# Attention on one core: the value products of a unit in five visits instead of nine, and the work beside them placed anew

## The chip, the cores and the metric

The kernel runs on one core of a Trainium2 chip. A core has a matrix engine (TensorE, in the profile PE, with its weight loads PEld), VectorE (DVE), ScalarE (ACT), GpSimd (POOL) and SyncE (SP, which issues most of the transfers). The engines run beside each other, each through its own instructions in their written order, and wait for each other through semaphores. The metric is the device time of one launch in microseconds (us).

## The reference

Attention over 8 batches and 8 heads of 576 positions with 64 columns, in which each query keeps its 32 largest scores, and then a layer of 8 experts over the 4608 positions, of which each position takes the one with the largest logit:

```
scores = scale * q @ k.T                        # scale = 1/8
kth    = 32nd largest score of each row
scores = where(scores >= kth, scores, -1e9)
attn   = exp(scores - max); attn /= sum(attn) + 1e-9
x      = attn @ v                               # heads side by side: 4608 x 512
logits = normalized(x) @ normalized(emb).T / tau
e      = argmax(logits); gate = softmax(logits)[e]
out    = gate * (relu(x @ w1[e]) @ w2[e])       # w1 512 x 1024, w2 1024 x 512
```

## The kernel before, in words

**Units and tiles.** Two batches and one head make a unit; there are 32 units (`NU`), eight to a pair of batches. A unit's 2 x 576 queries are nine tiles of 128 (tile 0 takes the last 64 queries of both batches, tiles 1 to 4 the first batch's others, 5 to 8 the second's), so there are 288 tiles. The attention stage is one loop, unrolled in Python, with one iteration `i` for each tile (line 1054), in which many steps for different tiles are issued; the order is written out by hand (`manual_schedule`), and each engine works through its part of it in that order. `m9` is `i % 9`; an iteration's number in the text is its `m9`.

**What an iteration issues.** On TensorE, in this order: the scores of tile i+2 (`nat`, L189: four matmuls of 288 columns, eight for a tile 0); in some iterations the expert columns of a unit (`expert_part`, L648); one chunk of the unit that was finished nine iterations ago (`chunk`, L885: the scores once more, but turned, so that keys are on the partitions, with a term that lies below zero for all keys under the threshold; chunk 4 of a unit holds the last keys of both batches and is issued in iteration 4 with twice the matmuls, its bf16 ones ending with 64 columns of weights); the value products (`av`, L898); and a piece of an early expert block. On ScalarE: L826 (sign against a first bound, with a count), L849 (`r`, what lies under the threshold), L794 (`xs`, the scores out of PSUM), L886 (`w`, the exponential of the chunk), and two times a unit L916 (`ob`, the copy of the finished products out of PSUM). On VectorE: eight maxima of L801 and the steps of L813 to L820 on them for the bound, L840 and L841 for the threshold. On GpSimd: L832 (one for each tile), and the splitting of queries and keys in two parts (L677, L679).

**Value products.** `av(u, b, c)` multiplies the weights `w` of chunk c of batch b with the values: 18 matmul instructions of 64 columns of weights and 73 columns (64 values, a one for the sum, 8 expert columns), which add up in one PSUM tile `po`. What is issued in one iteration is called a visit. Ten products a unit stand in nine visits, by the table `AVS` (lines 1049 to 1051): one in each iteration, two in iteration 6. The sums of batch 0 end in iteration 5 and are copied by `norm` in iteration 6, those of batch 1 end in iteration 0 and are copied in iteration 1. `winp`, nine constants that L841 reads on VectorE, is cut out of the same tile `po` (line 616).

**Expert columns.** `expert_part(u)` multiplies a unit's values with the expert embeddings (ten matmuls of 16 columns); `VES` lists the iterations in which it is issued, `load_vt` loads its input five iterations earlier into one of two buffers (`vt`), and `keep_ve` copies the kept result (`ves`) into the unit's values.

**Early expert blocks.** Once the positions of a pair of batches have been sorted to experts, 128 of an expert's positions can be worked through beside the attention. There are eight such blocks (`EARLY`), four of the first pair and four of the second, each with 17 pieces: one to turn the gathered rows (L473), eight up (L485) and eight down (L494).

**The planner.** It adds up for each iteration what it holds TensorE, ScalarE and GpSimd to be used (`used`, in ns) and carries what exceeds `SLOT` = 2950 as `debt`. A piece is placed where `spare("pe", 860)` finds room: debt, used and 860 within 2950. A visit counts 790, iteration 4's chunk 690 more, expert columns 1000. So pieces stand in all iterations but 4, 6 and those with expert columns. After the last tile, what is left of a segment is issued in one go (line 1109).

**Transfers.** SyncE issues them in order: `load` brings a unit's queries and keys, `stack` copies their split parts (`hi`, `lo`) to where the matmuls read them, `query_rows` and `top_row` build the second operand of the chunk, `load_v` and `load_vt` bring the values, and one expert weight transfer is issued in an iteration while there are any.

Of the kernel before, what the change touches and what calls it, by code (L numbers as in the profile page):

```python
# [10 lines left out]
F32 = mybir.dt.float32  # L11
F32R = mybir.dt.float32r
# [8 lines left out]
B, H, S, D = 8, 8, 576, 64  # L21
N, DM, E, F = B * S, H * D, 8, 1024
P = 128
SH = S // 2
NBP = B // 2
NU = NBP * H
# [25 lines left out]
def attn_moe_kernel(ctx: ExitStack, tc: tile.TileContext, qk, vb, vt, emb, tau, w1, w2, out):  # L52
# [537 lines left out]
    with ExitStack() as sx:  # L590
# [36 lines left out]
                nc.vector.memset(v[HALF[b], 8 + b, D:D + 1], 1.0)  # L627
            vts.append(v)
        vtr, ves = {}, {}
        VES = [6 + (7 * u) // 2 for u in range(NU)]  # L630

        def load_v(u):
            v, src = vts[u % NV], vb[u].rearrange("p (c d) -> p c d", c=9)
# [8 lines left out]
        def expert_part(u):  # L642

            h, t = u % H, vtr.pop(u)
            ve = ps_t.tile([P, 2, 512], F32, name=f"ve{u}", tag="pt")[:, 0, 0:10 * E].rearrange(
                "p (b c e) -> p b c e", b=2, c=5)
            for c in range(5):
                nc.tensor.matmul(ve[:, :, c], t[:, c * P:(c + 1) * P],  # L648
                                 eB[:, h].rearrange("p (b e) -> p b e", b=2),
                                 start=True, stop=True)  # L650
            ves[u] = vp.tile([P, 2, 5, E], F32, name=f"ves{u}", tag="ves", bufs=20)
            nc.scalar.copy(ves[u], ve)

        def keep_ve(u):
# [9 lines left out]
        QH = QW // 2  # L664

        def load(u, h):

            lo = sp.tile([P, QH], F32R, name=f"lo{u}_{h}", tag="lo", bufs=3)
            hi = sp.tile([P, QH], F32R, name=f"hi{u}_{h}", tag="hi", bufs=3)
            nc.sync.dma_start(lo.bitcast(F32), qk[u][:, QH * h:QH * h + QH])  # L670
            stage[u, h] = (hi, lo)

# [172 lines left out]

        def shut(i):
            r = rt[i] = wk.tile([P, S], BF16, name=f"r{i}", tag="rt" if i % 9 == 0 else "r",
                                bufs=2 if i % 9 == 0 else 10)
            nc.scalar.activation(r, xss.pop(i), AF.Relu, bias=tall[:, i:i + 1], scale=-1.0)  # L849

        ws = {}
# [1 line left out]
        def chunk(u, b, c):  # L853

            qs, kh, kl = stacks[u]
            w = ws[u, b, c] = wk.tile([P, S], F32, name=f"w{u}_{b}_{c}", tag="w", bufs=3)
            ps = ps_t.tile([P, 1024], F32, name=f"pt{u}_{b}_{c}", tag="pt")
            cut = (256, 320)[b]
            ps = ps[:, 512 - cut:512 - cut + S]
            part = [(0, cut), (cut, S)]  # L860
            for bb in ([b] if c < 4 else (1, 0)):
                first, offs = [], []
                k0, kn = (c * P, P) if c < 4 else ((512, 64), (448, P))[bb]
                rows = slice(0, kn)
                tiles = [(rt[u * 9 + 1 + 4 * bb + t], negi, P) for t in range(4)]
                tail = (rt[u * 9], negt[:, 64 * bb:64 * bb + 64], 64)
                tiles = tiles + [tail] if bb == 0 else [tail] + tiles
                q0 = 0 if bb == 0 else 640
                for kk, qq, n in ((kh, qs[:, q0:q0 + S], P), (kl, qts[u, bb], 65)):
                    for h0, h1 in part:  # L870
                        first.append((ps[rows, h0:h1], kk[0:n, bb * S + k0:bb * S + k0 + kn],
                                      qq[0:n, h0:h1], kk is kh, False))
                off = ([], [])
                o = 0
                for r, ni, n in tiles:
                    for hf, (h0, h1) in enumerate(part):
                        lo, hi = max(o, h0), min(o + n, h1)
                        if lo < hi:
                            off[hf].append((ps[rows, lo:hi], r[:, k0:k0 + kn],
                                            ni[:, lo - o:hi - o]))  # L880
                    o += n
                for hf in range(2):
                    offs += [(*x, False, n == len(off[hf]) - 1) for n, x in enumerate(off[hf])]
                for o_, l_, r_, start, stop in first + offs:
                    nc.tensor.matmul(o_, l_, r_, start=start, stop=stop)  # L885
            nc.scalar.activation(w, ps, AF.Exp, scale=0.125)  # L886
# [143 lines left out]
        debt = {"pe": 0, "act": 0, "pool": 0}  # L1030
        used = {}

        ROOM = {"pe": 0, "act": 1500, "pool": 1000}

        def spare(k, n, more=0):
            if i >= ntile or debt[k] + used[k] + n <= SLOT + ROOM[k] + more:
# [8 lines left out]
        for s in sorted(k for k in plan if k < 0):  # L1045
            for f in plan.pop(s):
                f()
        ok = lambda j: 0 <= j < ntile
        AVS = {1: [(0, 0, 1, 0)], 2: [(0, 1, 0, 0)], 3: [(0, 2, 0, 0)], 4: [(0, 3, 0, 0)],
               5: [(0, 4, 0, 1)], 6: [(1, 0, 1, 0), (1, 4, 0, 0)], 7: [(1, 1, 0, 0)],  # L1050
               8: [(1, 2, 0, 0)], 0: [(1, 3, 0, 1)]}
        i = -1
        while i < ntile + 12 or sideq or later or bankq or early or squares or wq or mo["seg"] \
                or mo["epi"]:
# [5 lines left out]
                used["pe"] += 712 + 690 * (m9 == 4)  # L1060
                used["act"] += 531
            avs = []
            for b, c, st_, sp_ in AVS[m9]:
                uu = w_ - (m9 == 0)
                if 0 <= uu < NU:
                    used["pe"] += 790
                    avs.append((uu, b, c, bool(st_), bool(sp_)))
            norms = [(w_ - (m9 == 1), (m9 == 1) * 1)] if m9 in (1, 6) else []
            norms = [x for x in norms if 0 <= x[0] < NU]
# [36 lines left out]
            if mo["seg"] is not None and not ntile <= i < ntile + 10 and spare("pe", 860):  # L1106
                todo, epi, after = mo["seg"]
                keep = KEEP if mo["of"] == 8 and i < ntile + 15 else 0
                for _ in range(max(len(todo) - keep, 0) if i >= ntile + 9 else 1):
                    lastpe.append(todo.pop(0))  # L1110
                if not todo:
                    mo["seg"], mo["epi"] = None, (epi, after)
# [619 lines left out]
```

## Time and profile before

| | |
|---|---|
| median of three runs | 1338.67 us (1338.01 to 1341.87) |
| profiled execution | 1340.78 us, its span 1339.0 us |
| TensorE busy over the span | 1281.6 us (96%), mean granted clock 0.974 |
| VectorE, ScalarE, GpSimd busy | 967.0 us (72%), 964.1 us (72%), 846.1 us (63%) |
| moved by DMA | 196.65 MB, mean 147 GB/s |

The page's busy tenths, in 40 slices of 33.5 us, show the stages: VectorE and ScalarE fall off where the attention ends.

```profile
PE   7999999999989999999999999999998999999997
DVE  7999999798878887888988888798834234443240
ACT  5899999898878898988889988898424234443231
POOL 5788888798877777888877887876522212122111
PEclk6899999899889999999999999999999999999999
```

A digit is the busy share of a slice in tenths, and of PEclk the granted clock of TensorE in tenths of full speed. Until 43.5 us the clock was mostly at half. The attention stage lasts to about 950 us, and the experts' stage follows. A busy share is an average over work with different limits, and the ends of matmuls are modelled, so that the time from the start of one group to the start of the next is what a group takes of TensorE.

### The profile page before, as it was taken

The page shows a single profiled execution, that of the slowest core. Times are in us where ns is not written, and L with a number is a line of the kernel's source. Part 1 is how long each engine was busy: PE and PEld are TensorE (multiplying, and loading weights), DVE is VectorE, ACT ScalarE, POOL GpSimd, SP SyncE. Part 2 cuts the span into 40 slices and gives each one's busy share as a digit, 9 for nine tenths or more (in the row PEclk, how much of TensorE's full clock was granted, in tenths as well). Part 3 has the DMA queues.
Part 4 walks back from the last instruction along what each step waited for, and adds up shares of the span by engine and source line. Part 5 has one row for each costly group of instructions (what it writes and reads, how often), then busy time and mean ns, then how long its engine had stood idle before and what let it go on. Part 6 is the DMA issues. An engine that isn't in the chain of part 4 may idle for free. (4 is left out here: it accounts for less than half of the span.)

```text
span 1339.0 us, 40065 instructions
## 1 busy us (share of the span) xinstructions
PE 1281.6 (96%) x13111; PEld 1126.4 (84%) x13111; DVE 967.0 (72%) x5961; ACT 964.1 (72%) x1890; POOL 846.1 (63%) x1413
## 2 busy tenths in 40 slices
PE   7999999999989999999999999999998999999997
PEld 5899999888878888888888988788797888888886
DVE  7999999798878887888988888798834234443240
ACT  5899999898878898988889988898424234443231
POOL 5788888798877777888877887876522212122111
PEclk6899999899889999999999999999999999999999
DMA  6477556644444667455666756550563325553201
GB/s 180 127 201 221 134 129 166 176 132 118 108 102 116 201 184 235 121 156 134 182 176 188 219 146 159 135 163 23 168 210 123 124 88 180 182 181 132 88 29 37
DMA packets 141174, 196.65 MB, mean 147 GB/s; under 512 B 66791, under 2 KB 67079, under 8 KB 140818
## 3 DMA queue, kind: packets, MB, share of 16 engines
q1 hardware_dynamic: 132626, 170.62, 45.8%
q0 software_dynamic: 8192, 22.07, 4.9%
q8 instruction: 127, 2.08, 0.7%
q14 instruction: 229, 1.88, 0.5%
HBM read 116.34 MB, written 20.87 MB: 102 GB/s over the span
## 5 line engine op out<-in xcount | busy, mean ns | idle before, releaser
L801 DVE MAX8 ca<-xs 128x8 f32<-128x72 f32 x2304 | 498.8, 221 | 2.3 <-ACT xs L794 1.6
L832 POOL TENSOR_TENSOR y<-xs,s 128x576 f32<-128x576 f32 x288 | 370.0, 1285 | 102.7 <-ACT s L826 45.3
L898 PE MATMUL po<-v,w 128*64 128x73 f32 x5760 | 270.2, 234 | 14.8 <-ACT ob L916 7.5
L189 PE MATMUL sc<-st 128*128 128x288 f32 (+1 forms) x1280 | 271.5, 341 | 7.5 <-DVE st L753 3.8
L898 PEld LDWEIGHTS po<-v,w 128*64 128x64 f32 x5760 | 227.2, 138 | 39.8 <-ACT s L826 7.2
L826 ACT ACTIVATE s<-xs,ball 128x576 bf16<-128x576 f32 x288 | 223.5, 776 | 21.4 <-DVE ball L820 11.5
L849 ACT ACTIVATE r<-xs,tall 128x576 bf16<-128x576 f32 x288 | 223.6, 777 | 14.4 <-DVE jk L841 11.2
L189 PEld LDWEIGHTS sc<-st 128*128 128x128 f32 (+1 forms) x1280 | 193.7, 198 | 48.0 <-issue 27.9
L840 DVE MAX8 z<-y 128x8 f32<-128x576 f32 x288 | 214.3, 744 | 20.6 <-POOL y L832 20.5
L886 ACT ACTIVATE w<-pt 128x576 f32<-128x576 f32 x288 | 187.9, 653 | 37.2 <-PE pt L885 31.5
L794 ACT ACTIVATE xs<-sc 128x576 f32<-128x576 f32 x288 | 185.8, 645 | 20.1 <-PE sc L189 19.0
L885 PE MATMUL pt<-st 128*128 128x256 f32 (+3 forms) x640 | 144.9, 308 | 0.3 <-ACT xs L794 0.3
L885 PE MATMUL pt<-qt,st 65*128 65x256 f32 (+3 forms) x640 | 139.1, 299 | 0.0
L841 DVE SCALAR_TENSOR_TENSOR jk<-po,c,z 128x9 f32<-128x9 f32 x288 | 65.7, 228 | 86.8 <-PE po L898 55.4
L885 PE MATMUL pt<-negi,r 128*128 128x128 bf16 (+2 forms) x1312 | 128.1, 222 | 0.0
L414 POOL DMA_INDIRECT out_dram<-ys_w,wi x20 | 24.8, 1240 | 159.6 <-ACT ys_w L1298 57.2
L679 POOL TENSOR_TENSOR lo<-lo,hi 128x202 fp32r<-128x202 f32 x186 | 115.7, 622 | 15.5
L885 PEld LDWEIGHTS <-r 128*128 128x128 bf16 (+1 forms) x1632 | 88.8, 101 | 28.2 <-issue 6.8
L885 PEld LDWEIGHTS pt<-qt,st 65*128 65x128 f32 (+1 forms) x640 | 104.2, 188 | 0.3
L885 PEld LDWEIGHTS pt<-st 128*128 128x128 f32 (+1 forms) x640 | 100.9, 189 | 1.9 <-ACT xs L794 0.6
L1279 PE MATMUL ph_w<-xTh,w 128*128 128x448 f32 (+3 forms) x384 | 96.5, 332 | 5.8 <-ACT w L546 3.4
L1294 PE MATMUL py_w<-w,hh 128*128 128x512 f32 x320 | 100.0, 393 | 0.8 <-ACT ys L1298 0.8
(288 smaller groups left out, 2360.2 us busy)
## 6 DMA issues: line engine op xcount, KB each, us to landing
r<-in_w SPq DMA_DIRECT2D x128, 256.0 KB
fr<-in_w SPq DMA_DIRECT2D x28, 1024.0 KB
lo<-in_qk SPq DMA_DIRECT2D x62, 304.0 KB
st<-hi SPq DMA_DIRECT2D x124, 152.0 KB
st<-lo SPq DMA_DIRECT2D x93, 152.0 KB
vt<-in_vt SPq DMA_DIRECT2D x32, 320.0 KB
qt<-st SPq DMA_DIRECT2D x64, 144.0 KB
st<-hi SPq DMA_DIRECT2D x62, 136.0 KB
```

What stands on the lines that cost most here:

```text
L189: nc.tensor.matmul(sc[:, hf, :SH], qs[0:r, cols(b)], kk[0:r, b * S + hf * SH:b * S + (hf + 1) * SH], start=(n == 0), stop=(n == len(terms) ...
L679: nc.gpsimd.tensor_tensor(lo[:, c], lo[:, c].bitcast(F32), hi[:, c].bitcast(F32), ALU.subtract)
L794: nc.scalar.mul(xs.rearrange("p (a b) -> p a b", a=2), scs.pop(i)[:, :, :SH], BIG)
L801: return [lambda gi=gi: nc.vector.max(out=ca[:, 8 * gi:8 * gi + 8], in_=xs[:, gi * GW:(gi + 1) * GW]) for gi in range(G)]
L826: nc.scalar.activation(s1, xss[i], AF.Sign, bias=ball[:, i:i + 1], scale=-DOWN, accum_out=c1)
L832: nc.gpsimd.tensor_tensor(y2, xss[i], s1s.pop(i), ALU.mult)
L840: lambda: nc.vector.max(out=z[:, 16:24], in_=y2),
L849: nc.scalar.activation(r, xss.pop(i), AF.Relu, bias=tall[:, i:i + 1], scale=-1.0)
L885: nc.tensor.matmul(o_, l_, r_, start=start, stop=stop)
L886: nc.scalar.activation(w, ps, AF.Exp, scale=0.125)
L898: nc.tensor.matmul(o, w[:, q:q + 64], vc, start=start and n < 2, stop=stop and n in (8, 7 - b))
L1294: nc.tensor.matmul(py, hi[:, f, col:col + P], wi[:, f, :], start=(n == 0), stop=(n == 3 * (F // P) - 1))
```

## The change

The ten products of a unit stand in five visits: two in iteration 2, one in 3, two in 5, two in 7 and three in 0 (of the next nine iterations). The sums end in iterations 5 and 0 as before. The planner counts a visit's first product at 900 and each further one at 570, and TensorE may run 500 over its slot. In iterations 1, 6 and 8, two pieces of a segment are issued where both find room. The expert columns go into iterations 1, 6 and 8 as well, three in nine iterations until 17 units' results are kept ahead, then one in nine. Four buffer counts differ: `ves` 19 instead of 20, `hi` 2 instead of 3, `r` 9 instead of 10, `w` 4 instead of 3.

```diff
@@ -627,7 +627,12 @@
                 nc.vector.memset(v[HALF[b], 8 + b, D:D + 1], 1.0)
             vts.append(v)
         vtr, ves = {}, {}
-        VES = [6 + (7 * u) // 2 for u in range(NU)]
+        VES = []
+        while len(VES) < NU:
+            n = VES[-1] + 1 if VES else 6
+            while n % 9 not in (1, 6, 8) or len(VES) - max(0, (n + 2) // 9) >= 17:
+                n += 1
+            VES.append(n)
 
         def load_v(u):
             v, src = vts[u % NV], vb[u].rearrange("p (c d) -> p c d", c=9)
@@ -648,7 +653,7 @@
                 nc.tensor.matmul(ve[:, :, c], t[:, c * P:(c + 1) * P],
                                  eB[:, h].rearrange("p (b e) -> p b e", b=2),
                                  start=True, stop=True)
-            ves[u] = vp.tile([P, 2, 5, E], F32, name=f"ves{u}", tag="ves", bufs=20)
+            ves[u] = vp.tile([P, 2, 5, E], F32, name=f"ves{u}", tag="ves", bufs=19)
             nc.scalar.copy(ves[u], ve)
 
         def keep_ve(u):
@@ -666,7 +671,7 @@
         def load(u, h):
 
             lo = sp.tile([P, QH], F32R, name=f"lo{u}_{h}", tag="lo", bufs=3)
-            hi = sp.tile([P, QH], F32R, name=f"hi{u}_{h}", tag="hi", bufs=3)
+            hi = sp.tile([P, QH], F32R, name=f"hi{u}_{h}", tag="hi", bufs=2)
             nc.sync.dma_start(lo.bitcast(F32), qk[u][:, QH * h:QH * h + QH])
             stage[u, h] = (hi, lo)
 
@@ -845,7 +850,7 @@
 
         def shut(i):
             r = rt[i] = wk.tile([P, S], BF16, name=f"r{i}", tag="rt" if i % 9 == 0 else "r",
-                                bufs=2 if i % 9 == 0 else 10)
+                                bufs=2 if i % 9 == 0 else 9)
             nc.scalar.activation(r, xss.pop(i), AF.Relu, bias=tall[:, i:i + 1], scale=-1.0)
 
         ws = {}
@@ -853,7 +858,7 @@
         def chunk(u, b, c):
 
             qs, kh, kl = stacks[u]
-            w = ws[u, b, c] = wk.tile([P, S], F32, name=f"w{u}_{b}_{c}", tag="w", bufs=3)
+            w = ws[u, b, c] = wk.tile([P, S], F32, name=f"w{u}_{b}_{c}", tag="w", bufs=4)
             ps = ps_t.tile([P, 1024], F32, name=f"pt{u}_{b}_{c}", tag="pt")
             cut = (256, 320)[b]
             ps = ps[:, 512 - cut:512 - cut + S]
@@ -1030,7 +1035,7 @@
         debt = {"pe": 0, "act": 0, "pool": 0}
         used = {}
 
-        ROOM = {"pe": 0, "act": 1500, "pool": 1000}
+        ROOM = {"pe": 500, "act": 1500, "pool": 1000}
 
         def spare(k, n, more=0):
             if i >= ntile or debt[k] + used[k] + n <= SLOT + ROOM[k] + more:
@@ -1046,9 +1051,8 @@
             for f in plan.pop(s):
                 f()
         ok = lambda j: 0 <= j < ntile
-        AVS = {1: [(0, 0, 1, 0)], 2: [(0, 1, 0, 0)], 3: [(0, 2, 0, 0)], 4: [(0, 3, 0, 0)],
-               5: [(0, 4, 0, 1)], 6: [(1, 0, 1, 0), (1, 4, 0, 0)], 7: [(1, 1, 0, 0)],
-               8: [(1, 2, 0, 0)], 0: [(1, 3, 0, 1)]}
+        AVS = {2: [(0, 0, 1, 0), (0, 1, 0, 0)], 3: [(0, 2, 0, 0)], 5: [(0, 3, 0, 0), (0, 4, 0, 1)],
+               7: [(1, 0, 1, 0), (1, 4, 0, 0)], 0: [(1, 1, 0, 0), (1, 2, 0, 0), (1, 3, 0, 1)]}
         i = -1
         while i < ntile + 12 or sideq or later or bankq or early or squares or wq or mo["seg"] \
                 or mo["epi"]:
@@ -1060,10 +1064,10 @@
                 used["pe"] += 712 + 690 * (m9 == 4)
                 used["act"] += 531
             avs = []
-            for b, c, st_, sp_ in AVS[m9]:
+            for b, c, st_, sp_ in AVS.get(m9, []):
                 uu = w_ - (m9 == 0)
                 if 0 <= uu < NU:
-                    used["pe"] += 790
+                    used["pe"] += 570 + 330 * (not avs)
                     avs.append((uu, b, c, bool(st_), bool(sp_)))
             norms = [(w_ - (m9 == 1), (m9 == 1) * 1)] if m9 in (1, 6) else []
             norms = [x for x in norms if 0 <= x[0] < NU]
@@ -1106,7 +1110,8 @@
             if mo["seg"] is not None and not ntile <= i < ntile + 10 and spare("pe", 860):
                 todo, epi, after = mo["seg"]
                 keep = KEEP if mo["of"] == 8 and i < ntile + 15 else 0
-                for _ in range(max(len(todo) - keep, 0) if i >= ntile + 9 else 1):
+                two = m9 in (1, 6, 8) and len(todo) > 1 and spare("pe", 860)
+                for _ in range(max(len(todo) - keep, 0) if i >= ntile + 9 else 1 + two):
                     lastpe.append(todo.pop(0))
                 if not todo:
                     mo["seg"], mo["epi"] = None, (epi, after)
```

## Rows read from the trace of the kernel before

**Rows 1.** Busy time by stretch: from:to, length, PE PEld DVE ACT POOL (instructions), PEclk, DMA.

```profile
43.50:225.00 181.50, 181.30 (x2366) 164.82 (x2367) 172.64 (x1222) 169.96 (x348) 146.64 (x249) 1.00 0.61 163
225.00:376.00 151.00, 143.99 (x1786) 130.18 (x1786) 131.84 (x928) 134.49 (x282) 130.00 (x234) 0.93 0.54 137
376.00:918.00 542.00, 528.36 (x6370) 458.13 (x6366) 454.81 (x3201) 473.99 (x934) 437.44 (x759) 0.99 0.59 160
```

**Rows 2.** Busy time by stretch, of line L832 alone, one instruction a tile.

```profile
43.50:225.00 181.50, 80.94 (x63) 1.00 0.61 163
225.00:376.00 151.00, 60.37 (x47) 0.93 0.54 137
376.00:918.00 542.00, 211.98 (x165) 0.99 0.59 160
```

**Rows 3.** TensorE in order: start us, us, operation; a plain iteration, 45.7 to 48.0 us.

```profile
45.72 0.81 PE L189 MATMUL sc<-st 128*128 128x288 f32 x4
46.36 0.43 PE L885 MATMUL pt<-st 128*128 128x256 f32 x2
...
47.14 0.19 PE L885 MATMUL pt<-negt,r 128*128 128x64 bf16 x1
47.26 0.85 PE L898 MATMUL po<-v,w 128*64 128x73 f32 x18
48.04 0.80 PE L189 MATMUL sc<-st 128*128 128x288 f32 x4
```

**Rows 4.** TensorE in order: iteration 6, a tile 0's scores, expert columns.

```profile
56.16 1.49 PE L898 MATMUL po<-v,w 128*64 128x73 f32 x36
57.58 1.34 PE L189 MATMUL sc<-st 128*128 128x288 f32 x8
58.76 1.19 PE L648 MATMUL ve<-eB,vt 128*128 128x16 f32 x10
59.80 0.39 PE L885 MATMUL pt<-st 128*128 128x320 f32 x1
```

**Rows 5.** TensorE in order: chunk and visit of an iteration 4.

```profile
50.38 0.39 PE L885 MATMUL pt<-negi,r 128*128 128x128 bf16 x5
50.57 0.45 PE L885 MATMUL pt<-st 128*64 128x256 f32 x2
...
51.22 0.41 PE L885 MATMUL pt<-negi,r 128*64 128x128 bf16 x4
51.42 0.28 PE L898 MATMUL po<-v,w 128*64 128x73 f32 x1
```

**Rows 6.** TensorE in order: an up piece, its scores up to the chunk.

```profile
420.96 1.16 PE L485 MATMUL bu4e<-bxe,r 128*128 128x128 f32 x8
...
422.50 0.42 PE L885 MATMUL pt<-st 128*128 128x320 f32 x2
```

**Rows 7.** Waits over the span: who waited for whom, us, times, longest us.

```profile
DVE jk L841 <- PE po L898: 55.4, 85, 5.8
...
PE po L898 <- ACT ob L916: 7.5, 8, 2.3
...
PE po L898 <- DVE ca L801: 6.5, 9, 1.6
...
PE bte L473 <- DMA xge<-xd,tgl: 4.8, 1, 4.8
```

**Rows 8.** Busy time by stretch, where the clock fell and where it didn't.

```profile
251.70:262.00 10.30, 10.30 (x75) 9.28 (x75) 6.52 (x48) 8.91 (x21) 6.96 (x13) 0.50 0.69 176
330.00:337.00 7.00, 4.71 (x65) 4.21 (x64) 4.51 (x35) 4.78 (x9) 5.48 (x8) 1.00 0.12 26
337.00:347.30 10.30, 10.10 (x73) 9.18 (x72) 6.66 (x42) 6.69 (x14) 9.54 (x15) 0.50 0.57 140
500.00:900.00 400.00, 391.27 (x4708) 337.06 (x4709) 338.19 (x2380) 351.88 (x697) 332.96 (x578) 1.00 0.63 170
```

**Rows 9.** TensorE in order: the pieces after the last visit.

```profile
943.86 6.28 PE L494 MATMUL bde<-r,bhe 128*128 128x512 f32 x14
```

## The prediction

> **What bounds the kernel now.** The page's slices show VectorE near full to about 900 of 1339 us, the attention stage, and that is where the change lies. There I read first the busy time by stretch, then TensorE's own order of instructions, then the waits. In the three stretches of the attention stage [rows 1] TensorE is busy 181.3 of 181.5 us, 144.0 of 151.0 and 528.4 of 542.0; the count of L832, one for each tile, says how many iterations each holds [rows 2]: 63, 47 and 165. An iteration so takes 2.88, 3.21 and 3.28 us. Per iteration VectorE is busy for 2.74, 2.81 and 2.76 us and ScalarE for 2.70, 2.86 and 2.87. TensorE is the limit in the first and the third stretch, by only 0.14 us in the first. In the second its clock stood at half for two spells of 10.3 us [rows 8], one of them right after a stretch in which it was idle for 2.3 of 7 us; there ScalarE's 2.86 is what would be left.
>
> VectorE's longest wait inside the stage (jk L841 for po L898, 55.4 us in 85 times [rows 7]) is no cause: `winp`, which L841 reads, is cut from the tile that the visits write, so L841 of an iteration waits for that iteration's visits, and the next visit waits for L841. It shows who is late, TensorE.
>
> **The price of a visit.** A plain iteration runs from one scores group to the next in 2.32 us [rows 3]: scores 0.64, chunk 0.90, visit 0.78. In iteration 6 two visits stand back to back and take 1.42 [rows 4], so a second one adds 0.64. What an iteration without a visit takes the trace doesn't show; I put it together. The eight scores matmuls of a tile 0 take 1.18 [rows 4], 0.54 more than four: after a visit four take 0.64, so 0.10 of it is the visit's. The chunk's last matmul (64 columns) starts 0.78 after its first and the visit only 0.12 after that [rows 3]; without a visit I let the scores follow after 0.03, since inside the chunk of iteration 4 an fp32r matmul follows the bf16 ones with no gap (five of them from 50.38, the next at 50.57 [rows 5]). That gives 0.81 + 0.54 = 1.35, so a visit costs 0.97, and one that is merged into another saves 0.97 - 0.64 = 0.33. From below the saving is 0 (the scores could pay the same after a chunk), from above 0.33; I take 0.33, as every part of it is a row.
>
> Four visits a unit are merged: those of iterations 1, 4, 6 and 8 go into 2, 5, 7 and 0 (that of 6 was double already and stays double). For iteration 4 I count nothing: its chunk ends in matmuls with 64 columns of weights, and there the visit starts beside them (51.42, the last bf16 ones being issued from 51.22 [rows 5]), so it pays no way in, and the way out to the scores is still to be paid without it. So 3 x 0.33 = 1.0 us a unit.
>
> [...]
>
> **First stretch, 43.5 to 225 us.** Seven units at 25.93 us. Minus 1.0; plus the expert columns, one of which takes 1.04 (58.76 to 59.80 [rows 4]): three in nine iterations instead of two in seven, 0.43 more a unit, 0.45 us. 25.38 a unit is 2.82 an iteration, 0.08 above VectorE: 3.9 us saved, of which I take 3, two engines at nearly the same load never running quite at the larger one's. Ends: -3.2 (no saving, the columns paid) and +8.9 (VectorE's own 172.6).
>
> **Second stretch, 225 to 376.** The old list puts 12 expert parts here (76 to 114), the new one 6 (78, 80, 89, 98, 107, 116). TensorE loses 6 x 1.04 and 5.2 x 1.0 of its 144.0, some 132.6 us, and ScalarE's 134.5 is the floor. The copy of `po` (L916) and the first visit of the next half stood in the same iteration (1 and 6), and TensorE waited for it 7.5 us in 8 times, up to 2.3 [rows 7]; now an iteration lies between (copy 1, visit 2; copy 6, visit 7). One such wait came right ahead of the fall of the clock at 337 us [rows 8]. A fall costs half of 10.3, 5.15 us. But iterations without a visit or a piece also leave TensorE idle, by up to 2.9 - 1.35 = 1.5 us at once, so I let one of two falls stay: 134.5 + 5.1 + 3.8 for waits between ScalarE and the others = 143.4, 7.6 saved. Ends: 16.5 (the floor) and -5.2 (one fall more).
>
> **Third stretch, 376 to 918.** The merged visits give 18.3 x 1.0 = 18.3. Against that stand the pieces. By the planner's budgets the old kernel places one in seven iterations of nine (none in 4 and 6); the new one two in 1, 6 and 8 where a segment has two left, one in 3 and 4, none in 0, 2, 5 and 7. Worked through with its debts that is about 7.5 a unit, and all 136 end near iteration 285, so the seven down pieces that ran after the last visit [rows 9] and one more come in here: 8 x 0.87 = 7.0. An up piece with its scores takes 1.54 [rows 6], 0.90 over a plain iteration's scores, and a down piece much the same (fourteen of its matmuls, seven pieces, last 6.3 us, their end modelled: 0.87 to 0.90 each [rows 9]); standing without a visit, the 0.10 by which the scores start late is the piece's own. That is 0.10 for about 55 iterations (in 4 the chunk's end pays it, in 3 the visit): 5.5. Its way in from a bf16 chunk isn't shown: between 0 (fp32r after bf16 [rows 5]) and 0.19 (the 0.09 by which a visit starts late in rows 3, and 0.10 for a slow first matmul); I take 0.05, near the row without a change of weight columns: 2.7. The second of a pair costs what a piece cost. Two expert parts (125, 134) are new here: 2.1. So TensorE's work falls by 18.3 - 7.0 - 5.5 - 2.7 - 2.1 = 1.0 only. It also waited 13.6 us; the 4.8 for the first gathered block [rows 7] stay, and of the other 8.8, which are mostly visits that wait for the copy or for L841, I let 4 go. 5 saved. Ends: -16 (merging saves half, the way in 0.19, no wait gone) and +12 (no way in, all 8.8 gone).
>
> **The rest.** After the last visit TensorE did the seven down pieces (6.3 us [rows 9]) beside the last gate's chain on ScalarE, GpSimd and VectorE; taking them away shortens nothing, and it leaves TensorE idle there. 1.0 for the last unit's visits against a slower restart: 0. At the start, with the clock at half until 43.5 us, a third expert part falls into iteration 10: -1. The expert stage is not touched.
>
> At nothing I cost the buffers. `r` with nine: tile 6 of a unit takes the place of tile 5 of the unit before, read last two iterations earlier. `w` with four: in program order each is read ahead of the chunk that takes its place. `hi` with two: six iterations (17 us) lie between the copies out of it and its next writing on GpSimd; if they were late, GpSimd's products (L832) would queue behind. `vt` keeps two buffers while each third load is now issued an iteration before the matmuls that free its place, so SyncE waits there with the top rows behind it; these are due three iterations on. Without that cover it would be up to an iteration's 2.8 us, nine times.
>
> The three visits of iteration 0 last 0.78 + 2 x 0.64 = 2.06 us, and L841 of that iteration waits for them: they fit into VectorE's 2.74 if they start in its first 0.7. Where TensorE is the limit this costs nothing.
>
> **Sum.** 3 + 7.6 + 5 + 0 - 1 = 14.6 us. The profiled execution took 1340.78 (span 1339.0 and 1.8 around it); it is 2.1 over the median of the three runs, to which I apply the sum: 1338.67 - 14.6 = 1324.
>
> **The rivals.**
> The pieces eat it. The way in is 0.19 (7.7 more in 55 iterations), no wait goes (4) and VectorE and TensorE get into each other's way in the first stretch (3): 1324 + 14.7 = 1339, no change. For: the new price of a piece is the one thing no row shows. Against: bf16 to fp32r is free.
>
> All of it. VectorE's floor in the first stretch (5.9 more), ScalarE's in the second (8.9), no way in and no waits in the third (7.5): 1302. For: both large stops ahead of the falls hang on the copy that gets an iteration's distance. Against: 0.08 us between two engines.
>
> The clock. TensorE is busy almost throughout now [rows 1]; with the visits gone from four iterations of nine it stands idle where no piece is to be had, in the second stretch and in the 6 us after the last visit. Each fall takes 5.15 us; 2.8 more than I count eat the gain, 3.6 make it 0.3% slower; four give 1345. For: a stop of 2.3 us was enough ahead of 337. Against: from 500 to 900 us, with waits of up to 1.6 us [rows 7], it stayed whole [rows 8]. [...]
>
> Merging saves nothing. A visit by itself would cost no more than its 0.64 and the rest be the scores' and the chunk's own; then the first stretch pays 3.2 instead of gaining 3 and the third loses its 18.3: 1324 + 24.5 = 1348. Against: 1.42 is well under two times 0.78 plus two late starts [rows 3, 4]. [...]
>
> **Chances.** Forecast 0.48 (1316 to 1332), pieces 0.18, all of it 0.16, clock 0.13, no saving 0.05. A change under 0.3% (4 us) can't be told from none. Faster: 0.48 + 0.16 + 0.03 of the pieces = 0.67; same 0.15; slower 0.18. The range reaches from the second rival to just above the first: 1302 to 1341.
>
> **What would show it.** L898 still with 5760 matmuls, in five groups a unit; a double visit of 1.42 and a triple one near 2.06; scores of 0.54 right after a chunk. Iterations of about 2.82 in the first 63. No wait of `po` for `ob` over 1 us. Down pieces over before the last visit. One or no spell at half clock between 225 and 376 us. Wrong if scores or pieces after a chunk start 0.1 or more late, if L841's wait grows beyond its 55 us in the first stretch, or if the clock's mean falls below the 0.974 of now.

## The result, and the profile after

The changed kernel takes 1350.49 us (median of 6 runs, 1346.02 to 1352.41), the kernel before beside it 1340.27 (6 runs, 1337.86 to 1342.65): a ratio of 1.0075, 95% interval [1.0054, 1.0096]. It is 10 us slower where 14.6 faster was forecast, and lies above the range of 1302 to 1341. The profiled execution took 1352.41.

Busy time by stretch in the changed kernel, cut where the same tiles' products (L832, now L837) begin; columns as in [rows 1]:

```profile
44.44:224.58 180.14, 180.12 (x2399) 166.38 (x2399) 170.98 (x1215) 169.22 (x351) 145.93 (x249) 0.99 0.62 170
224.58:371.71 147.13, 132.46 (x1724) 118.18 (x1722) 131.64 (x927) 133.05 (x275) 130.20 (x237) 0.97 0.50 129
371.71:926.32 554.61, 530.78 (x6391) 463.80 (x6392) 454.52 (x3201) 473.66 (x938) 435.94 (x757) 0.98 0.58 158
```

The third of these stretches in the last kernel of the table below (a_nob_pad, an experiment):

```profile
374.91:911.01 536.10, 526.69 (x6392) 460.11 (x6392) 454.59 (x3202) 473.31 (x938) 436.46 (x756) 0.99 0.60 163
```

The same tiles give, for three kernels (the last is a_nob_pad), in us:

| | start | first | second | third | from there to the end |
|---|---|---|---|---|---|
| before | 43.48 | 181.64 | 151.56 | 541.73 | 420.57 |
| forecast change | +1 | -3 | -7.6 | -5 | 0 |
| after | 44.44 | 180.14 | 147.13 | 554.61 | 424.37 |
| after, both causes taken away | 44.78 | 182.48 | 147.65 | 536.10 | 416.39 |

Each measured row is one execution. The times of one kernel spread by 5 to 13 us; a_nob_pad's profiled execution was 3.9 us under the median of its kernel and that of the changed kernel 1.9 over.

The first two stretches gained, 5.9 us of the 10.6 forecast. The third lost 12.9, and TensorE's work in it hardly grew (530.8 against 528.4 [rows 1]): it stands still for 23.8 us instead of 13.6, and without the two causes for 9.4. What follows lost 3.8. The waits of the changed kernel (who, for whom, us, times, longest), in which the wait of `po` for `ob` [rows 7] is no longer found:

```profile
DVE jk L846 <- PE po L903: 69.8, 63, 6.5
...
PE pt L890 <- ACT xs L799: 20.6, 18, 3.3
...
PE pr L369 <- DVE ohba L233: 6.1, 1, 6.1
...
POOL hi L682 <- DMA qt<-tr: 5.8, 1, 5.8
...
POOL hi L682 <- DMA lo<-in_qk: 5.2, 5, 3.9
...
PE sc L189 <- DMA st<-lo: 4.1, 2, 3.8
```

The waits of TensorE and GpSimd for `st`, `lo` and `qt` took 7.9 us in the kernel before; here they take 20. One costly place, first in SyncE's queue of transfers (start, us until the last is issued, line, how many), then on TensorE, on GpSimd, and by stretch:

```profile
728.38 4.83 SPq L967 DMA_DIRECT2D r<-in_w  x7
733.32 1.78 SPq L705 DMA_DIRECT2D st<-hi  x3
735.20 1.35 SPq L705 DMA_DIRECT2D st<-lo  x2
```

```profile
738.80 2.00 PE L485 MATMUL bu0e<-bxe,r 128*128 128x128 f32 x16
744.58 1.31 PE L189 MATMUL sc<-st 128*128 128x288 f32 x8 [3.77 <-DMA st<-lo]
```

```profile
745.49 0.37 POOL L682 TENSOR_SCALAR hi<-lo 128x202 fp32r<-128x202 f32 x1 [3.88 <-DMA lo<-in_qk]
...
746.53 1.27 POOL L837 TENSOR_TENSOR y<-xs,s 128x576 f32<-128x576 f32 x1
```

```profile
724.00:740.00 16.00, 16.00 (x205) 14.79 (x204) 15.28 (x112) 15.73 (x35) 12.33 (x24) 1.00 0.77 204
740.00:746.10 6.10, 2.33 (x19) 2.17 (x18) 3.23 (x21) 3.13 (x8) 1.96 (x6) 1.00 1.05 315
746.10:749.50 3.40, 3.40 (x44) 3.02 (x42) 0.00 (x0) 1.94 (x4) 3.15 (x5) 0.50 1.01 367
```

Seven transfers of an expert's down weights, 256 KB each, go out in one go just ahead of the next unit's stack. They are issued from 728.38 us on, the stack's five from 733.32, and the DMA engines' share is 1.05 from 740.0 to 746.1; the scores of the unit's tile 0 wait 3.77 us for `st`, GpSimd stands 3.88 at a copy into `hi` with the products (L837) behind it, and the granted clock is 0.50 for the 3.4 us from 746.1. In the program such a burst comes from `weights`: the first up piece of a block issues whatever of its expert's weights still waits in `wq`, the down weights too, which nothing needs before the eight up pieces are done. The kernel before has bursts as well; the new places of the pieces move them to other iterations of the unit.

The largest of TensorE's waits listed above is not for `st` but for `xs`; 8.9 us of it are four waits in the third stretch. One of these comes after the burst at 592 us (seven transfers as well). GpSimd stands for 4.95 us at the copy of the kept expert columns into `v`, which the profile puts down to one of GpSimd's own transfers; its products follow late, and ScalarE and TensorE wait in their turn:

```profile
601.48 0.19 POOL L665 COPY v<-ves 64x8 f32<-64x8 f32 x1 [4.95 <-DMA lst<-enta,slotia]
604.11 0.78 ACT L831 ACTIVATE s<-xs,ball 128x576 bf16<-128x576 f32 x1 [4.81 <-POOL y L837]
607.00 0.53 PE L890 MATMUL pt<-st 128*128 128x256 f32 x2 [2.48 <-ACT xs L799]
```

In the third stretch GpSimd waits at this copy for some 20 us, against 4.3 in the kernel before.

The second place is in the expert stage, where no line was changed: TensorE's idle time ahead of an up matmul, and the branch of the first `Switch` (count, ns least/median/most, start), in the changed kernel, then the branch in the one before:

```profile
999.49 0.55 PE L1266 MATMUL ph<-xTh,w 128*128 128x256 f32 x1 [4.07 <-issue]
```

```profile
L1733 PEldq COMPARE_BRANCH  x1: 5267/5267/5267, 993.9 to 993.9; - x1
```

```profile
L1728 PEldq COMPARE_BRANCH  x1: 362/362/362, 989.9 to 989.9; - x1
```

### The profile page after: what moved, and what is told of

Its sections match the earlier page's. It is cut to its first block, busy times and chain, and to the rows that moved or that the text cites. A ratio compares the mean times of both kernels' runs of the same rounds, so it can differ in the third digit from the quotient of the medians.

```text
span 1350.7 us, 39910 instructions
## 1 busy us (share of the span) xinstructions
PE 1267.5 (94%) x13111; PEld 1123.0 (83%) x13111; DVE 966.1 (72%) x5961; ACT 960.1 (71%) x1890; POOL 842.2 (62%) x1413
## 5 line engine op out<-in xcount | busy, mean ns | idle before, releaser
L837 POOL TENSOR_TENSOR y<-xs,s 128x576 f32<-128x576 f32 x288 | 369.2, 1284 | 92.6 <-ACT s L831 52.2
L189 PE MATMUL sc<-st 128*128 128x288 f32 (+1 forms) x1280 | 265.0, 335 | 11.7 <-DVE st L758 4.2
L903 PE MATMUL po<-v,w 128*64 128x73 f32 x5760 | 244.2, 234 | 6.9 <-DVE jk L846 3.9
L903 PEld LDWEIGHTS po<-v,w 128*64 128x64 f32 x5760 | 220.2, 140 | 22.3 <-DVE jk L846 5.6
L189 PEld LDWEIGHTS sc<-st 128*128 128x128 f32 (+1 forms) x1280 | 190.8, 197 | 45.1 <-issue 19.0
L799 ACT ACTIVATE xs<-sc 128x576 f32<-128x576 f32 x288 | 185.5, 644 | 11.2 <-PE sc L189 10.8
L414 POOL DMA_INDIRECT out_dram<-ys_w,wi x20 | 21.6, 1078 | 163.5 <-ACT ys_w L1303 61.6
```

What stands on the lines that cost most here:

```text
L189: nc.tensor.matmul(sc[:, hf, :SH], qs[0:r, cols(b)], kk[0:r, b * S + hf * SH:b * S + (hf + 1) * SH], start=(n == 0), stop=(n == len(terms) ...
L799: nc.scalar.mul(xs.rearrange("p (a b) -> p a b", a=2), scs.pop(i)[:, :, :SH], BIG)
L837: nc.gpsimd.tensor_tensor(y2, xss[i], s1s.pop(i), ALU.mult)
L903: nc.tensor.matmul(o, w[:, q:q + 64], vc, start=start and n < 2, stop=stop and n in (8, 7 - b))
```

## The experiments

Each kernel was timed in five rounds against the kernel before on the same chip; ratios are to that, with 95% intervals. Three groups: the bursts, the parts of the change, the branch.

**a_nob: the changed kernel without bursts.** A piece sends off only the weights that it reads itself; the others go one an iteration.

```diff
-        def weights(e):
-            for k in range(2):
-                while any(x[:2] == (k, e) for x in wq):
-                    wq.pop(0)[2]()
-            return wts[0, e], wts[1, e]
+        def weights(e, k):
+            while any(x[:2] == (k, e) for x in wq):
+                wq.pop(0)[2]()
+            return wts[k, e]
```

> The changed kernel, with one edit: a piece that needs an expert's first weights no longer issues what is still waiting of that expert's second weights. Theory 1 (the loss comes from bursts of six or seven weight transfers of 256 KB, which the new places of the pieces put ahead of the next unit's stack transfers and top rows): TensorE's waits for st and qt at 470, 675, 745 and 888 us and GpSimd's of 4 to 6 us for hi go, and the kernel is 8 to 14 us faster than the changed one, 1336 to 1342 us, at or under the kernel before. Theory 2 (two buffers of hi instead of three make GpSimd wait for the copies out of it): no change, 1348 to 1352. Theory 3 (the visits themselves, bunched, make the engines wait for each other): no change either.

1337.71 us, 0.9991 [0.9973, 1.0009]: 11 us under the changed kernel by the ratios. No burst of four or more is left, TensorE waits for no `st`, and the waits at `hi` are down from 13.0 us to 1.7. So taking the bursts away takes the loss away. GpSimd still waits 18.4 us at the copy into `v` in the third stretch, but for 3.0 at most instead of 5.0, and TensorE's four waits for `xs` there are down from 8.9 us to 4.8; what makes GpSimd stop there without bursts was not tested.

**b_nob: the kernel before with the same edit.**

> The kernel before, with the same edit. It has the bursts too, eight transfers each, but only two of its seven come one or two iterations ahead of a unit's second stack transfers. Theory 1: 0 to 4 us faster than before (GpSimd's waits for hi of 4.6 and 3.3 us go). Theories 2 and 3: within 2 us of before.

1335.0, 0.9986 [0.9973, 0.9999]: its own bursts cost it 1.9 us only. They stand elsewhere in the units.

**a_hi3: the changed kernel with three buffers for `hi`**, and for room 16 for the expert columns, which moves their list and with it the blocks.

```diff
-            hi = sp.tile([P, QH], F32R, name=f"hi{u}_{h}", tag="hi", bufs=2)
+            hi = sp.tile([P, QH], F32R, name=f"hi{u}_{h}", tag="hi", bufs=3)
```

> The changed kernel with three buffers of hi; for the room, the expert columns are kept 14 units ahead instead of 17 with 16 buffers instead of 19 (three expert parts move some 30 iterations later, at most 3 us). Theory 1: 1347 to 1353, as the changed kernel; TensorE's waits for st and qt stay. Theory 2: 1337 to 1343, GpSimd's waits of 1.9, 5.8 and 3.9 us before hi go and TensorE's behind them. Theory 3: 1347 to 1353.

1341.52, 1.0034 [1.0015, 1.0054], in the range given for the buffers. GpSimd waits hardly any more at `hi` (0.7 us at most), but TensorE does for the transposed queries, in three places:

```profile
PE pt L890 <- DMA qt<-tr: 6.2, 3, 3.9
```

Since the bursts moved too, the run doesn't tell the buffer's share from theirs.

**b_hi2: the kernel before with two buffers for `hi`.**

> The kernel before with two buffers of hi instead of three and nothing else. Theory 2: 5 to 10 us slower than before, with more waits of GpSimd before hi than the 7.9 us of now. Theories 1 and 3: within 2 us of before.

1337.45, 0.999 [0.9977, 1.0002]: in the kernel before two buffers cost nothing. Whether a third would soften the bursts of the changed kernel stays open.

**a_b2 and a_b7: bursts put on purpose.** On top of a_nob, the eight down weights of an expert are held and sent off together, at the end of iteration 2 of a unit, or of iteration 7.

```diff
-            if wq and i >= 0:
+            if wq and i >= 0 and (wq[0][0] == 0 or m9 == 2 or i >= ntile):
                 wq.pop(0)[2]()
+                while wq and wq[0][0] == 1 and m9 == 2 and i < ntile:
+                    wq.pop(0)[2]()
```

> The changed kernel without its own bursts, but with bursts made on purpose: the eight down weights of an expert are held and sent off together at the end of the first iteration 2 of a unit that comes. Same bytes, same pieces, same visits as the next run; only the place in the unit differs. If a burst costs where it stands just ahead of the transfers of the next unit's stack (as at 457 and 728 us of the changed kernel), TensorE waits for a stack or a transposed query, or GpSimd for hi, in each unit with a burst: some 3 to 6 us each in four or five of seven units, 1348 to 1360, and over 8 us above the next run. If bursts cost by themselves, wherever they stand, or not at all: within 3 us of the next run.

> As the run before it, but the eight weights are sent off at the end of iteration 7 of a unit. If the place decides, a burst here comes after the stack of the next unit has been loaded and is through before the next loads: the time of the same kernel without bursts, 1336 to 1340. If bursts cost by themselves: as the run before it.

In iteration 2: 1369.43, 1.024 [1.021, 1.027], above the range expected. In iteration 7: 1344.99, 1.0045 [1.0026, 1.0063]. One of the bursts in SyncE's queue, first of a_b2 with what GpSimd does after it, then of a_b7:

```profile
736.30 4.76 SPq L967 DMA_DIRECT2D r<-in_w  x8
741.17 1.78 SPq L705 DMA_DIRECT2D st<-hi  x3
```

```profile
753.44 0.37 POOL L682 TENSOR_SCALAR hi<-lo 128x202 fp32r<-128x202 f32 x1 [3.87 <-DMA lo<-in_qk]
```

```profile
729.11 2.02 SPq L705 DMA_DIRECT2D st<-hi  x3
...
743.48 3.76 SPq L967 DMA_DIRECT2D r<-in_w  x8
747.34 0.70 SPq L720 DMA_DIRECT2D qt<-st  x1
```

Against a_nob, by the ratios, the same bytes in eight bursts (one of them in the first stretch) cost 33 us ahead of the stack and 7 behind it. The place decides most of it; that a burst in iteration 7 would be free was wrong. There GpSimd stands at the copy into `v` for up to 6.2 us, and TensorE waits for `xs` in four places of the third stretch, 11.2 us in all.

**a_oldpc: the pieces where they were.** The changed kernel's visits, list and buffers, with each piece in the iteration in which the kernel before issues it (the planner's costs and due times of before).

```diff
-                two = m9 in (1, 6, 8) and len(todo) > 1 and spare("pe", 860)
-                for _ in range(... else 1 + two):
+                for _ in range(... else 1):
```

> The changed kernel with one thing undone: each piece of the early blocks is issued in the iteration in which the kernel before issues it (one at most, seven iterations of nine, seven of the last down pieces after the last visit); the merged visits, the new list of expert columns and the buffers stay. Theory 1 (the loss comes from the weight bursts, set off by a block's first up piece, where they stand just ahead of the next unit's stack transfers): the bursts return to the places of before, TensorE waits for no stack or transposed query for more than 1.5 us, and the gain of 7 us of the first 400 us stays to the end: 1326 to 1333. Rival 2 (merged visits themselves make VectorE and ScalarE late, wherever the pieces stand): no better than 1339. Rival 3 (the pieces brought in from the tail cost it, bursts or not): also 1326 to 1333, but then the same kernel without bursts gains nothing more.

1344.86, 1.0035 [1.0016, 1.0055], outside what was expected. The later experiments on the branch explain a part of the difference, some 6 of at least 12 us: this kernel has the long branch too (4.54 us), which I took at that time for part of the tail. The bursts, back at the places of before, explain another part (next run).

**a_oldpc_nob: that, without bursts.**

> As the run before it, and a piece sends off only the weights that it reads itself, so that no burst is left. Theory 1: the bursts of the kernel before cost it some 4 us (as taking them away from it showed), so this is 3 to 5 us below the run before it, 1322 to 1329, and the best so far. Rival 2: within 2 us of the run before it, and not under 1335.

1338.58, 0.999 [0.9971, 1.0008]: the same as a_nob, and not the 1322 to 1329 that I expected. Without bursts no difference shows between the two placings of the pieces, the seven down pieces of the tail among them. With the pieces where they were, the bursts cost 6.0 us by the ratios, 1.9 in the kernel before and 11.2 at their new places; differences of this kind are good to some 3 us. So their new places are a part of what the bursts cost, and whether merged visits make them dearer at the old places too isn't settled.

**a_nob_keep: seven down pieces kept for the tail**, on top of a_nob.

```diff
+            held = i < ntile and not bankq and not early and mo["seg"] is not None \
+                and mo["of"] == 8 and len(mo["seg"][0]) <= 7
-            if mo["seg"] is not None and not ntile <= i < ntile + 10 and spare("pe", 860):
+            if mo["seg"] is not None and not held and not ntile <= i < ntile + 10 \
+                    and spare("pe", 860):
```

> The changed kernel without bursts, with its own places for the pieces, except that the last seven down pieces wait until after the last visit, as in the kernel before. It tells what the empty tail costs. If TensorE's 4.5 us of standing still ahead of the last ranks, the half clock after it and the stop of 5.2 us near 980 us come from the missing pieces: 5 to 9 us below the same kernel without this edit (1337.7), 1329 to 1333. If the tail's chain on ScalarE, GpSimd and VectorE hides the pieces as I forecast, then only the six us of pieces leave the attention stage: 1331 to 1334, with the stop near 980 us still there. No change (1336 to 1339) if the third stretch isn't limited by TensorE.

1341.88, 1.0005 [0.9985, 1.0024]: no gain from keeping them. The idle time ahead of the last ranks (the 6.1 us in the waits above) costs nothing that shows, and the stop in the expert stage stays (its branch took 5.28 us).

**b_ves: the kernel before with the new list of expert columns only.**

> The kernel before with only the list of the iterations with expert columns exchanged for the new one (three in nine iterations at first, then one in nine and fewer). It prices that part by itself. Each expert part takes TensorE about 1.04 us; two more fall into the first stretch and six leave the second. If TensorE's work is all that matters: first 225 us +3, second stretch -5 or more, the whole 1334 to 1338. If SyncE's wait for the place of the next value tile holds up the stacks' transfers: slower, 1341 to 1345.

1345.22, 1.0037 [1.0022, 1.0052]: 5 us slower. To the end of the first stretch it loses 6.2 us: 1.0 before it begins, 5.1 in it,

```profile
44.53:231.29 186.76, 186.76 (x2393) 170.29 (x2394) 172.90 (x1224) 172.50 (x351) 146.80 (x249) 0.98 0.62 164
```

where I had counted 3.1 for the three parts more. The six parts that leave the second stretch give 1.7 back, up to 380 us, not 6.2: there TensorE isn't the limit. (The transfers' part of that expectation wasn't told apart.)

**a_nob_pad: the branch moved.** On top of a_nob, 75 small matmuls in TensorE's idle 4.4 us of the start. They move its instructions by 150. Counted in the trace, the first `Switch`'s branch is TensorE's instruction 23,105 in the kernel before, 22,961 in the changed one, 22,955 in a_nob: merged visits issue 144 semaphore instructions less (354 for 498).

```diff
+        for n in range(75):
+            nc.tensor.matmul(po[:, 0:8], onesb, onesb[:, 0:8], start=True, stop=True)
```

> The changed kernel without bursts, with 75 matmuls of eight columns after the first 17 ones of the start, where TensorE stands idle for 4.4 us (6.9 to 11.3 us). They shift TensorE's instructions by 150, to where the kernel before has them: the changed kernels issue some 145 semaphore instructions less. The branch of the expert stage's first Switch took TensorE 4.5 to 6.4 us in all six profiled kernels with merged visits and under 0.4 in the four without. If it is the place of the instructions that decides, the branch is short again, the expert stage begins 4 to 7 us sooner, and the time is 1330 to 1334. If it depends on the load on the DMA engines or on the clock, the branch stays at 4.5 us or more and the time at 1336 to 1340.

1333.11, 0.9949 [0.9931, 0.9968]: faster than both kernels. The branch is short:

```profile
L1734 PEldq COMPARE_BRANCH  x1: 361/361/361, 978.5 to 978.5; - x1
```

**a_nob_pad_v27: with the old pace of expert columns** until 17 are waiting.

```diff
-            n = VES[-1] + 1 if VES else 6
-            while n % 9 not in (1, 6, 8) or len(VES) - max(0, (n + 2) // 9) >= 17:
+            n = 6 + (7 * len(VES)) // 2
+            while len(VES) - max(0, (n + 2) // 9) >= 17 or n in VES:
```

> As the run before it, with the expert columns at the old pace (two in seven iterations, at any place in the unit) until 17 are waiting, and after that one a unit. The kernel before lost 5 us by the new list alone, 6.2 of them in the first 225 us, where six more parts stand. If the parts are TensorE's work and nothing else, this gains 5 to 6 us in the first 225 and gives back up to 3 after: 2 to 5 us below the run before it. If merged visits leave iterations into which a part fits for less, the new list is no loss here: within 1 us.

1333.36, 0.9947 [0.9929, 0.9964]: no difference. Beside merged visits the new list costs nothing that shows; beside nine visits it cost 5 us.

**a_pad: the changed kernel with 72 such matmuls and nothing else.**

> The changed kernel with nothing but 72 small matmuls in TensorE's idle 4.4 us of the start, which put its instructions where the kernel before has them; bursts and pieces as they are. If the place of the instructions is a cause of its own, beside the bursts: the branch of the first Switch under 0.5 us instead of 5.27, and the time 4 to 7 us under the changed kernel's 1350, 1343 to 1347, with the attention stage ending as late as there (within 3 us of 950). If the gain of the padded kernel without bursts came from something else (a warmer start, chance): 1348 to 1352 and a branch of 4 us or more.

1339.8, 1.0026 [1.0008, 1.0045], under what was expected. Its attention stage ended at 944.7, earlier than the 947 allowed, and by its ratio it is 6.6 us under the changed kernel. From the start of the branch to that of the next long one it takes 41.1 us, the changed kernel 47.9. The branch:

```profile
L1735 PEldq COMPARE_BRANCH  x1: 357/357/357, 988.3 to 988.3; - x1
```

**b_pad: the kernel before with 56**, 112 instructions, to 23,217, which is 256 after the changed kernel's place.

> The kernel before with 56 such matmuls, 112 instructions, which move its instructions to where the changed kernels have theirs, if places 256 instructions (or 128, or 64) apart are alike; that period is a guess. If so: the branch takes 4 us or more, and the time is 1343 to 1347. If the period is another one, the branch may stay short and the time within 2 us of before; then only the padded changed kernels show the cause.

1345.29, 1.0058 [1.0035, 1.0081], 7.8 us slower, with nothing added but the small matmuls at the start, which move every later instruction:

```profile
L1730 PEldq COMPARE_BRANCH  x1: 4831/4831/4831, 989.5 to 989.5; - x1
```

## Why the prediction was wrong

Two steps failed, each for something that the sum put at nothing. With both taken away (a_nob_pad) the change gives 0.9949, 6.8 us, and some 5 against the kernel before without its own bursts (b_nob, 0.9986): also then less than half of the 14.6 forecast. The bursts cost 10.3 (a_pad against a_nob_pad) or 11.2 (the changed kernel against a_nob), the branch 6.6 (the changed kernel against a_pad) or 5.6 (a_nob against a_nob_pad). These are differences of ratios that were taken in different sessions, each good to some 3 us.

**"At nothing I cost the buffers", and with them the transfers.** Here the sum lost most. I followed the moved pieces on TensorE and left out what they issue: the first up piece of a block flushes its expert's waiting weights into SyncE's queue, ahead of the stack that the next unit begins with. I had written what would happen if `hi` came late (GpSimd's products behind it), but put it at nothing and looked for its cause in the number of buffers; b_hi2 shows that two cost the kernel before nothing, a_nob that without bursts GpSimd waits only 1.7 us at two, and a_b2 against a_b7 that bursts are dear where they stand ahead of the stack (33 us against 7). And `hi` isn't the only place: GpSimd's stops at the copy into `v`, which the sum didn't have at all, hold up the products too (4.95 us at 601). In the rows at 728 us the stack's five transfers were issued behind the seven of weights, and the waits after them were 3.77 us for TensorE and 3.88 for GpSimd.

**"The expert stage is not touched."** No line of it was, but its place in TensorE's instructions was. The first branch took 0.36 us at 23,099 to 23,113 (seven kernels: three of those with padding, and before, b_nob, b_hi2 and b_ves) and 4.5 to 6.4 us at 22,955 to 22,966 and at 23,217 (nine kernels). a_pad and b_pad turn it off and on (0.36 us instead of 5.27, 4.83 instead of 0.36). From the start of this branch to that of the next long one it is 40.8 to 41.2 us in the seven kernels and 46.1 to 48.7 in the nine; what follows takes 306 to 310 us in all of them. So the long branch costs the kernel 5 to 8 us by the traces, as by the ratios. b_pad, put 256 behind the changed kernel's place, has a long branch too (4.83 us); whether places repeat with a period, as guessed for it, these runs don't show. The shortest of TensorE's 16 branches of that line (L1733) took 0.31 us in the changed kernel.

**The price of a visit: right in kind, the sum too high.** TensorE in the changed kernel, a double, scores right after a chunk, a triple and no visit:

```profile
53.61 1.48 PE L903 MATMUL po<-v,w 128*64 128x73 f32 x36
55.02 0.80 PE L189 MATMUL sc<-st 128*128 128x288 f32 x4
...
63.79 0.79 PE L189 MATMUL sc<-st 128*128 128x288 f32 x4
64.41 0.43 PE L890 MATMUL pt<-st 128*128 128x256 f32 x2
...
65.31 2.13 PE L903 MATMUL po<-v,w 128*64 128x73 f32 x54
67.36 0.81 PE L189 MATMUL sc<-st 128*128 128x288 f32 x4
...
407.57 0.81 PE L189 MATMUL sc<-st 128*128 128x288 f32 x4
...
409.02 2.00 PE L485 MATMUL bu4e<-bxe,r 128*128 128x128 f32 x16
410.78 1.32 PE L189 MATMUL sc<-st 128*128 128x288 f32 x8
```

The double takes 1.41 us and the triple 2.05, as forecast. Scores right after a chunk take 0.62, not 0.54: their late start isn't the visit's alone, and this is the part of the price that was mis-sized. An iteration without a visit takes 1.45 up to its pieces, not 1.35, so a visit costs 2.32 - 1.45 = 0.87 by itself and a merged one saves 0.23, not 0.33. Nor do 18 of these matmuls take the same wherever they stand, as the last rival had it: 0.64 behind others, 0.87 by themselves. Two up pieces take 1.76, so the way in to them isn't dear. A unit still reaches 2.83 us an iteration (72 to 225 us), against 2.82 forecast, at TensorE's limit.

**First stretch** (-3): -1.5 in the changed kernel, +0.8 in a_nob_pad, where two units ran at 2.97 and 2.95 and the others at 2.83 to 2.84 after the first.

**Second** (-7.6): -4.4 and -3.9, of which some may be chance, since b_nob, with the visits and pieces of before, has 148.8 us there for before's 151.6. TensorE's work fell by 11.5, as I had it, to 132.5; the other terms gave less than I took.

**Third** (-5): -5.6 without the two causes, in an execution 3.9 us under its kernel's median; TensorE's work fell by 1.7 and its waits by 4.2, where the sum had 1.0 and 4. But other kernels with merged visits and no bursts gave -5.3 (a_nob), -4.0 (a_nob_keep), -1.2 (a_nob_pad_v27) and +1.8 (a_oldpc_nob), and b_nob, with no visit merged, -2.7. So that the size was right isn't shown, and two of its terms were too large (merging, the way in).

**Start** (+1): +0.96. **Rest** (0): +3.8, for the branch wasn't in it. With the branch as short as before it is -4.2 (a_nob_pad), 4.0 of that ahead of the branch. The pieces that left the tail may be that: a_nob_keep, which holds seven of them there, takes 3.9 longer than a_nob from the end of the third stretch to the branch. By the times a_nob_keep's 1.9 us over a_nob can't be told from none, so that taking them away shortens nothing isn't shown.

Of the rivals none was the cause, but the clock is part of the price. Its mean fell below 0.974, to 0.968, which I had named as a sign of being wrong. In the third stretch TensorE stood at half clock for 20.4 us in five spells, in the kernel before for 6.8 in one and in a_nob_pad for 10.2 in two. I had looked for falls where no piece is to be had; those at 483, 609, 746 and 879 us come with waits of TensorE of 2.0 to 3.8 us, three of them for `xs` and that at 746 for `st`, and that at 999 comes behind the branch.

## What to carry to other kernels

When a step is moved, list the DMAs it sets off and see what it overtakes in the issuing queue: here the kernel that issued its weights one an iteration (a_nob) took 11 us less than that with bursts, and a flush belongs at least behind the transfers that the next stage begins with: eight bursts cost 33 us ahead of them (a_b2) and still 7 behind them (a_b7). And a change that only removes semaphores still moves every later instruction of an engine (144 fewer here, with 5 to 8 us at one branch): before two versions are compared by less than a per cent, look at the branches of both, and pad one until they agree.

## What was not expected of the hardware

The branch of the first `Switch` on TensorE took 0.36 us or 4.5 to 6.4 by its place among the instructions (0.36 at 23,105 in the kernel before, 5.27 at 22,961 in the changed one). The prefetch hint was issued 13.9 us ahead (980.0 against 993.9) in the changed kernel, where it was long, and 13.8 in a_pad, where it was short. A later branch, at 1041.8 us there, took 5.3 to 6.6 us in every profiled kernel, moved by the padding or not. One near 1200 us goes the other way: it took 1.8 to 3.6 us in the seven kernels in which the first is short and 0.32 in the nine others. Why a place is long isn't shown.
